# Agent attention with routed experts on one core: GpSimd's chain instructions in halves, strays marked, threshold set and expert loaded later, tiles 13 to 15 of three batches as float16 pairs

## The chip, the cores and the metric

One core of a Trainium2 chip runs the whole program. The metric is the device time of one execution in microseconds (us). Its engines are TensorE (PE in the profile, its weight loads PEld), VectorE (DVE), ScalarE (ACT), GpSimd (POOL) and SyncE (SP), which only issues transfers. Each engine takes its instructions in one fixed order.

## What is computed

For each of B = 4 batches of N = 11456 rows of width 128 there is attention through A = 49 agents, and after it a mixture of E = 8 experts in which each row goes to one expert:

```python
a2k = sm(agents, k); agent_v = a2k @ v          # sm: softmax of scaled scores
x = sm(q, agents) @ agent_v                      # then all batches as rows x
logits = normalized(x) @ normalized(emb).T / tau
e = argmax(logits); gate = softmax(logits)[e]
out = gate * (relu(x @ w1[e]) @ w2[e])           # D = 128, F = 1024
```

## The kernel before, in words

**Tiles.** A batch is 23 tiles (NT) of 4 x 128 rows, the last of 2 x 96; two tiles make a unit, the piece that is loaded, transposed and scored at once. A tile has TICKS = 4 ticks, a tick two half-steps. Every stage is a generator that yields the half-steps to wait (an argument `g` of `pick_expert` is 0 for batch 0 and 1 for the others), and the order in which they emit instructions is the priority from which a scheduler, with times of its own, fixes each engine's order before anything runs. SP's order is exactly the order of emission. `tc.issue_after` (through `in_place`) puts an instruction behind another on the same engine.

**The expert chain.** `pick_expert` runs once per batch, beside the tiles of the batch before (for batch 0 ahead of all tiles). All rows of a batch are expected at one expert, and its hidden units are ordered so that two blocks of 128 are computed exactly and the others are taken as linear: `load_expert` (L885 to L889) loads w1 and w2 into w1s and w2s (one buffer each, SP's queue). The hidden weights gp (L710) give ordering keys (L755 to L770, small DVE operations). From them come diag (L772, POOL for batches 1 to 3), nkey and sgn (L774, L775, DVE), the matmuls `row` (L784), the ranks (L793, L795), the selection sel (L801), and gh and gl (L809 to L819), without which the tiles of this batch do not begin. POOL also makes the low half of gt (L790), scales w2s (L735) and makes the low half of w2x (L736). The linear part lin (L838 to L846) and the placed second layer w2p (L856 matmuls, L858 copied on DVE) follow, then an all-partition maximum (`allmax`: transpose mT L214, DVE reduction mTx L216, matmul mB L219), the threshold thr (L871), 8 instructions sel (L875) and vm (L880). vm serves the proofs.

**Tiles of the expert.** `ffn_mm1` makes hp (L1211, L1212) and the hidden hh. For tiles under LATE = 13, and for all of batch 3, hh is a pair of float16 (ACT L1220, DVE L1221), and `ffn_mm2` does three float16 products per hidden block f (2) and 128 rows (4): L1247 to L1249. Tiles from 13 on of batches 0 to 2 (`plain`) keep hh in float32 (ACT L1216) and do one float32 product with w2f (L1244), which the chip issues as two instructions. L1235 adds the linear part, `ffn_out` scales on DVE (ot, L1263) and stores.

**Proofs and strays.** `proved` (L1056, L1059, L1062, L1065) checks that the linear part holds for each row; `mark_strays` (L1082 to L1182, small DVE operations and L1084 on POOL) marks rows that fail or go to another expert, after the batch's last proof and, half-way, once the next batch has its w2p. `fix` computes a batch's marked rows again: it loads the expert, gathers the rows (`gather`, POOL), waits 24 half-steps and runs `answer` (L1351 with w1s, L1357 with w2s). `stray_first` runs `stray` once, with a load of its own, before fix of batches 2 and 3.

**Other work in the same engines.** Units of q are transposed on PE (L425), scored (L438) and exponentiated, split by POOL (e, L931), transposed by a DMA of SP's queue (tt, L935) and routed (L946, L947). Units of k for batches 2 and 3 are half of them split into float16 pairs (`k1_pairs`, L489 on DVE).

## Time and profile before

| what | value |
|---|---|
| median of three runs | 700.36 us (696.67 to 705.64) |
| the profiled execution: its time / its span | 699.89 us / 698.1 us |
| PE, DVE, ACT, POOL busy | 652.2, 535.5, 453.6, 355.1 us |
| mean granted TensorE clock | 0.969 |

The span runs from the first to the last instruction; 1.8 us lie around it. A clock of 1.0 is the level of 2.4 GHz, 0.5 the level of 1.2 GHz. Batch 0's tile 0 is scaled (ot) at 102 us, its tile 22 at 255, batch 1's at 429, batch 2's at 575, batch 3's at 688.

### The profile page before, as it was taken

The numbers are of one execution on the slowest core, as the hardware profiler recorded it, in microseconds if no ns is written. First come the engines' busy times: TensorE is split into PE (matmuls) and PEld (weight loads), VectorE is DVE, ScalarE is ACT, GpSimd is POOL, SyncE is SP. The second block draws the span as 40 slices with busy tenths as digits, with TensorE's granted clock in tenths as the row PEclk, the third lists the DMA queues.
The fourth block names the chain that finished last, engine by engine and source line by source line (L and its number), as shares of the span: only waits on it lengthen the run. The fifth ranks groups of instructions, "written<-read, shape, count | busy, mean of one in ns | idle before, by whom it ended". The sixth has DMA issues, their size and how long they took to land. (4 is left out here: it accounts for less than half of the span.)

```text
span 698.1 us, 23174 instructions
## 1 busy us (share of the span) xinstructions
PE 652.2 (93%) x9227; PEld 557.9 (80%) x9227; DVE 535.5 (77%) x1470; ACT 453.6 (65%) x1127; POOL 355.1 (51%) x606
## 2 busy tenths in 40 slices
PE   8998999999998888989999888999999999996996
PEld 6886888888887767878889677888888798775876
DVE  5767796878686988876767888977657889985983
ACT  3538746966887636847688853776577857992632
POOL 6002382675153745873533484685645656876410
PEclk9999999999999989989999997999999999998999
DMA  8995596699692267996959245998575424205141
GB/s 342 281 341 174 133 287 169 144 277 238 204 252 69 62 173 194 303 255 160 256 147 221 83 106 136 267 279 204 151 170 169 113 65 114 59 17 171 54 147 70
DMA packets 157047, 123.16 MB, mean 176 GB/s; under 512 B 76787, under 2 KB 133191, under 8 KB 156939
## 3 DMA queue, kind: packets, MB, share of 16 engines
q1 hardware_dynamic: 143499, 97.97, 55.5%
q10 hardware_dynamic: 13120, 23.47, 9.7%
q8 instruction: 73, 1.20, 0.7%
q14 instruction: 35, 0.29, 0.1%
q0 software_dynamic: 320, 0.24, 0.1%
HBM read 80.26 MB, written 23.79 MB: 149 GB/s over the span
## 5 line engine op out<-in xcount | busy, mean ns | idle before, releaser
L1065 ACT ACTIVATE vp<-vp 128x512 f32<-128x512 f32 x180 | 106.1, 590 | 18.7 <-PE vp L1056 13.1
L1220 ACT ACTIVATE hh<-hp 128x512 f16<-128x512 f32 (+1 forms) x124 | 72.4, 591 | 51.7 <-PE hp L1212 30.7
L438 PE MATMUL sp<-aT_all,fT 128*64 128x49 f32 x2496 | 96.4, 226 | 3.4 <-DVE avx L543 2.0
L1221 DVE SCALAR_TENSOR_TENSOR hh<-hp,hh 128x512 f16<-128x512 f32 (+1 forms) x124 | 82.9, 674 | 21.1 <-ACT hh L1220 18.6
L438 PEld LDWEIGHTS sp<-aT_all,fT 128*64 128x64 f32 x2496 | 84.3, 139 | 16.3 <-issue 3.6
L1247 PE MATMUL yp<-w2p,hh 128*128 128x128 f16 (+1 forms) x492 | 95.0, 223 | 0.1
L1248 PE MATMUL yp<-w2p,hh 128*128 128x128 f16 (+1 forms) x492 | 94.9, 223 | 0.0
L1249 PE MATMUL yp<-w2p,hh 128*128 128x128 f16 (+1 forms) x492 | 93.7, 223 | 0.0
L1056 PE MATMUL vp<-vm,tt 128*128 128x256 f16 x360 | 71.0, 274 | 3.9 <-DVE vmin L1062 2.3
L931 POOL TENSOR_TENSOR e<-qe,e 128x392 f16<-128x392 f32 (+1 forms) x48 | 42.2, 880 | 63.3 <-ACT e L928 62.2
L1211 PE MATMUL hp<-tt,gh 128*128 128x512 f16 (+1 forms) x184 | 69.5, 378 | 3.9 <-DVE hh L1221 1.6
L1263 DVE TENSOR_TENSOR ot<-yp,gs 128x512 f32<-128x512 f32 (+1 forms) x92 | 61.2, 668 | 14.6 <-PE yp L1244 8.7
L430 ACT COPY fT<-fTp 128x512 f32<-128x512 f32 (+1 forms) x103 | 57.0, 569 | 23.6 <-PE fTp L425 19.7
L1006 POOL TENSOR_TENSOR nrm<-qq,half 128x16 f32<-128x16 f32 (+2 forms) x28 | 69.9, 2498 | 0.2
L1212 PE MATMUL hp<-tt,gl 128*128 128x512 f16 (+1 forms) x184 | 69.3, 377 | 0.0
L1235 PE MATMUL yp<-lin,tt 128*128 128x128 f16 x720 | 64.9, 224 | 4.5 <-DVE ot L1263 4.4
L1244 PE MATMUL yp<-w2f,hh 128*128 128x128 f32 (+1 forms) x456 | 66.3, 283 | 0.0
L1244 PEld LDWEIGHTS yp<-w2f,hh 128*128 128x128 f32 (+1 forms) x456 | 60.0, 195 | 4.3 <-issue 0.8
L1235 PEld LDWEIGHTS <-tt 128*128 128x128 f16 x720 | 51.1, 102 | 12.3 <-issue 6.0
L425 PE MATMUL fTp<-ident,qt 128*128 128x128 f32 x360 | 55.0, 284 | 1.2 <-ACT hh L1216 0.9
L1247 PEld LDWEIGHTS <-hh 128*128 128x128 f16 (+1 forms) x492 | 49.4, 100 | 4.4 <-ACT hh L1220 0.3
L963 POOL TENSOR_TENSOR rt<-qe 128x392 f32<-128x392 f32 (+1 forms) x48 | 38.4, 800 | 28.2 <-ACT qe L923 20.1
(371 smaller groups left out, 1713.3 us busy)
## 6 DMA issues: line engine op xcount, KB each, us to landing
kt<-in_k_dram SPq DMA_DIRECT2D x44, 512.0 KB, 5.9
vt<-in_v_dram SPq DMA_DIRECT2D x44, 512.0 KB, 7.3
qt<-in_q_dram SPq DMA_DIRECT2D x44, 512.0 KB, 5.2
out_dram<-ot ACTq DMA_DIRECT2D x88, 256.0 KB, 2.3
w1s<-in_moe_w_dram SPq DMA_DIRECT2D x9, 512.0 KB, 5.2
w2s<-in_moe_w_dram SPq DMA_DIRECT2D x9, 512.0 KB
tt<-e SPq DMA_TRANSPOSE x48, 5.2
kt<-in_k_dram SPq DMA_DIRECT2D x4, 96.0 KB, 3.8
```

The lines of the kernel that those rows point to most:

```text
L438: pe.matmul(out=s[h : h + w, c * A : (c + 1) * A], lhsT=xT[:, c * p + h : c * p + h + w], rhs=aT_all[:, b, :], start=True, stop=True, skip ...
L1006: pool.tensor_tensor(out=nrm, in0=quad, in1=half[:, :n], op=ALU.pow)
L1056: pe.matmul(out=z[:p, i * FP : (i + 1) * FP], lhsT=tt[:, c * p : (c + 1) * p], rhs=bt.vm[:, LO:], start=True, stop=True)
L1065: act.activation(z[:p], z[:p], AF.Relu, scale=-1.0, accum_out=bt.vsum[:p, at : at + 1])
L1211: pe.matmul(out=hp[:, :m], lhsT=bt.gh[:, fs], rhs=tt, start=True, stop=False)
L1220: h_last[:] = [act.activation(hh[:, :m], hp[:, :m], AF.Relu)]
L1221: dve.scalar_tensor_tensor(out=hl[:, :m], in0=hp[:, :m], scalar=0.0, in1=hh[:, :m], op0=ALU.max, op1=ALU.subtract)
L1235: pe.matmul(out=yp[:p, c, :], lhsT=tc_, rhs=bt.lin[:, h], start=(c == 0 and h == 0), stop=False, skip_group_check=True)
L1244: y_last[:] = [pe.matmul(out=y, lhsT=hh[:, cs], rhs=bt.w2f[:, f], start=False, stop=last, skip_group_check=True)]
L1247: pe.matmul(out=y, lhsT=hh[:, cs], rhs=wh, start=False, stop=False, skip_group_check=True)
L1248: pe.matmul(out=y, lhsT=hh[:, cs], rhs=wl, start=False, stop=False, skip_group_check=True)
L1249: y_last[:] = [pe.matmul(out=y, lhsT=hl[:, cs], rhs=wh, start=False, stop=last, skip_group_check=True)]
```

## The change

Tiles 13 to 15 of batches 0 to 2 become float16 pairs (LATE 16). The POOL instructions L735, L736, diag and the low half of gt are issued as two halves each, and for batches 1 to 3 L735, L736 and gt stand behind diag in POOL's order; nkey and sgn are emitted before diag. w2p of batches 1 to 3 is copied by ACT. For those batches the transpose mT starts two half-steps later, mB three more, both behind the last emitted product of `ffn_mm2` on PE, and so thr, L875 and vm follow five half-steps later. `mark_strays` waits for the next batch's vm instead of its w2p. `fix` gathers first and loads the expert after its 24 half-steps. L489 is issued in two halves.

```diff
--- before.py
+++ after.py
@@ -43,7 +43,7 @@
     AT = {0: 0, 2: 1}
     BRISK = 4
     KEEP = 5
-    LATE = 13
+    LATE = 16
 
     REM_J, REM_P = 2, 96
     J = (N - REM_J * REM_P) // P
@@ -208,15 +208,18 @@
             except StopIteration as s:
                 return s.value
 
-    def allmax(col, n, tag, psx, g, bufs=2):
-
+    def allmax(col, n, tag, psx, g, bufs=2, place=None):
+
+        place = place or nullcontext
         t_ = psx("mT")
-        pe.transpose(out=t_[:n, :P], in_=col, identity=ident)
+        with place():
+            pe.transpose(out=t_[:n, :P], in_=col, identity=ident)
         mx = sm.tile([P, 1], F32, name="mTx", tag="mTx")[:n]
         dve.tensor_reduce(out=mx, in_=t_[:n, :P], axis=AX.X, op=ALU.max)
         yield g
         t_ = psx("mB")
-        pe.matmul(out=t_[:, :n], lhsT=mx.broadcast_to([n, P]), rhs=ident[:n, :n], start=True, stop=True)
+        with place():
+            pe.matmul(out=t_[:, :n], lhsT=mx.broadcast_to([n, P]), rhs=ident[:n, :n], start=True, stop=True)
         r = sm.tile([P, n], F32, name="pm", tag=tag, bufs=bufs)
         act.copy(r, t_[:, :n])
         return r
@@ -486,7 +489,9 @@
             pool.tensor_tensor(out=src[:p, :n], in0=src[:p, :n], in1=sc.unsqueeze(2).broadcast_to([p, n, D]), op=ALU.mult)
             pool.tensor_tensor(out=xs[:p, :n, 1], in0=src[:p, :n], in1=xs[:p, :n, 0], op=ALU.subtract)
         else:
-            dve.scalar_tensor_tensor(out=xs[:p, :n, 1], in0=src[:p, :n], scalar=sc, in1=xs[:p, :n, 0], op0=ALU.mult, op1=ALU.subtract)
+            for c in range(0, n, TJ):
+                cs = slice(c, min(c + TJ, n))
+                dve.scalar_tensor_tensor(out=xs[:p, cs, 1], in0=src[:p, cs], scalar=sc, in1=xs[:p, cs, 0], op0=ALU.mult, op1=ALU.subtract)
         used("k", b, u)
         yield 6
         i = yield from take(x_slots)
@@ -732,11 +737,21 @@
             yield g
             act.activation(w2x[:, :, 0], w2s, AF.Copy, scale=s3)
             if b > 0:
-                pool.tensor_tensor(out=w2s, in0=w2s, in1=s3.unsqueeze(2).broadcast_to([P, NF, D]), op=ALU.mult)
-                pool.tensor_tensor(out=w2x[:, :, 1], in0=w2s, in1=w2x[:, :, 0], op=ALU.subtract)
+                for h in halves:
+                    with in_place(made):
+                        pool.tensor_tensor(out=w2s[:, h], in0=w2s[:, h], in1=s3.unsqueeze(2).broadcast_to([P, NF // 2, D]), op=ALU.mult)
+                        pool.tensor_tensor(out=w2x[:, h, 1], in0=w2s[:, h], in1=w2x[:, h, 0], op=ALU.subtract)
             return s3, i3
 
         mean, key, nkey, sgn, pw = col("mean"), col("key"), col("nkey"), col("sgn"), col("pw")
+
+        made = []
+        halves = [slice(0, NF // 2), slice(NF // 2, NF)]
+
+        def signs():
+
+            dve.tensor_scalar(nkey, key, -1.0, None, ALU.mult)
+            dve.tensor_scalar(sgn, mean, 0.0, -0.5, ALU.is_ge, ALU.add)
 
         def order_keys():
 
@@ -769,10 +784,13 @@
             yield 1
             dve.tensor_tensor(out=ki, in0=ki, in1=uid, op=ALU.bitwise_or)
             yield 1
-            vec.tensor_tensor(out=diag, in0=ident.unsqueeze(1).broadcast_to([P, NF, P]),
-                              in1=key.unsqueeze(2).broadcast_to([P, NF, P]), op=ALU.mult)
-            dve.tensor_scalar(nkey, key, -1.0, None, ALU.mult)
-            dve.tensor_scalar(sgn, mean, 0.0, -0.5, ALU.is_ge, ALU.add)
+            if b > 0:
+                signs()
+            for h in halves:
+                made[:] = [vec.tensor_tensor(out=diag[:, h], in0=ident.unsqueeze(1).broadcast_to([P, NF // 2, P]),
+                                             in1=key[:, h].unsqueeze(2).broadcast_to([P, NF // 2, P]), op=ALU.mult)]
+            if b == 0:
+                signs()
 
         i2 = yield from (beside(order_keys(), first_scale()) if b == 0 else beside(first_scale(), order_keys()))
         if b > 0:
@@ -787,7 +805,10 @@
             act.copy(row[:, hs], t_)
             yield g
 
-        pool.tensor_tensor(out=gs_[1], in0=gg, in1=gs_[0], op=ALU.subtract)
+        for h in halves:
+            with in_place(made) if b > 0 else nullcontext():
+                pool.tensor_tensor(out=gs_[1][:, 2 * h.start : 2 * h.stop], in0=gg[:, 2 * h.start : 2 * h.stop],
+                                   in1=gs_[0][:, 2 * h.start : 2 * h.stop], op=ALU.subtract)
         rank, more = col("rank"), col("more")
         for c in range(NF // 2):
             dve.tensor_scalar(junk[0], row, key[:, c : c + 1], 0.0, ALU.is_lt, ALU.add, accum_out=rank[:, c : c + 1])
@@ -855,7 +876,7 @@
                 for c in range(NF):
                     pe.matmul(out=t_[:, k_ * 2 * D : (k_ + 1) * 2 * D], lhsT=sel[:, c, (f + k_) * P : (f + k_ + 1) * P],
                               rhs=w2x[:, c].rearrange("p h d -> p (h d)"), start=(c == 0), stop=(c == NF - 1))
-            (act.copy if f % 4 else dve.tensor_copy)(w2p[:, f : f + nk].rearrange("p f h d -> p (f h d)"), t_[:, : nk * 2 * D])
+            (act.copy if b > 0 else dve.tensor_copy)(w2p[:, f : f + nk].rearrange("p f h d -> p (f h d)"), t_[:, : nk * 2 * D])
             yield g
         bt.w2p = w2p
         iall = sm.tile([P, 1], F32, name="iall", tag="iall")
@@ -865,7 +886,8 @@
         bt.iall = iall
         dve.tensor_scalar(rank, rank, -float(FM), None, ALU.add)
         yield 1
-        top = yield from allmax(gmx, 2, "gmxr", psx, 1)
+        yield 2 * g
+        top = yield from allmax(gmx, 2, "gmxr", psx, 1 + 3 * g, 2, lambda: in_place(y_last if b > 0 else []))
         thr = sm.tile([P, 1], F32, name="thr", tag="thr")
         bt.far = sm.tile([P, 1], F32, name="far", tag="far")
         dve.tensor_scalar(thr, top[:, :1], 1.05 * 2.0 ** -11, None, ALU.mult)
@@ -1086,7 +1108,7 @@
         idx = sm.tile([P, NCOL], F32, name="idx", tag="idx", bufs=1)
         dve.tensor_reduce(out=idx, in_=oh, axis=AX.X, op=ALU.min)
         yield 1
-        while b < B - 1 and not hasattr(batches[b + 1], "w2p"):
+        while b < B - 1 and not hasattr(batches[b + 1], "vm"):
             yield 1
         odd = sm.tile([P, NCOL], F32, name="odd", tag="odd", bufs=1)
         ne = sm.tile([P, NCOL], F32, name="ne", tag="ne", bufs=1)
@@ -1376,9 +1398,10 @@
         dve.tensor_scalar(none, bt.fix[:, :1], 0.5, 2 * BIG, ALU.is_lt, ALU.mult)
         yield 1
         dve.scalar_tensor_tensor(out=ix, in0=bt.fix[:, :1], scalar=-1.0, in1=none, op0=ALU.add, op1=ALU.add)
+        xq = gather(ix)
+        yield 24 if b < B - 1 else 0
         w1s, w2s = load_expert(bt.e0i)
-        xq = gather(ix)
-        yield 24 if b < B - 1 else 8
+        yield 0 if b < B - 1 else 8
         yield from answer(xq, ix, bt.fix[:, 1:], aT_all[:, b], av_all[:, b], w1s, w2s, (b + 1) * NT)
         bt.fixed = True
```

## Rows read from the trace of the kernel before

**Rows 1.** The page, part 1: busy us (share of the span) xinstructions of an engine.
```profile
PE 652.2 (93%) x9227; PEld 557.9 (80%) x9227; DVE 535.5 (77%) x1470; ACT 453.6 (65%) x1127; POOL 355.1 (51%) x606
```

**Rows 2.** Busy time by stretch: us, each engine's busy us, clock, DMA share, GB/s.
```profile
147.00:182.00 35.00, 34.96 (x571) 30.50 (x568) 26.18 (x59) 24.59 (x61) 16.63 (x24) 1.00 1.01 238
182.00:205.00 23.00, 23.00 (x301) 20.85 (x300) 15.03 (x49) 18.22 (x46) 8.07 (x13) 1.00 0.91 251
...
510.00:529.50 19.50, 19.50 (x231) 17.65 (x230) 11.50 (x42) 15.73 (x41) 8.68 (x14) 1.00 0.91 226
```

**Rows 3.** Timeline of PE: start, us, instruction; eight float32 instructions, eight float16 products, one.
```profile
207.87 1.05 PE L1244 MATMUL yp<-w2f,hh 128*128 128x128 f32 x8
...
613.37 0.61 PE L1235 MATMUL yp<-lin,tt 128*128 128x128 f16 x8
...
615.30 0.22 PE L1247 MATMUL yp<-w2p,hh 128*128 128x128 f16 x1
```

**Rows 4.** The page, part 5: group | busy us, mean ns | idle before, releaser.
```profile
L1221 DVE SCALAR_TENSOR_TENSOR hh<-hp,hh 128x512 f16<-128x512 f32 (+1 forms) x124 | 82.9, 674 | 21.1 <-ACT hh L1220 18.6 <-issue 1.9
...
L1244 PE MATMUL yp<-w2f,hh 128*128 128x128 f32 (+1 forms) x456 | 66.3, 283 | 0.0
```

**Rows 5.** Timeline of batch 1's keys, DVE, POOL and PE: start, us, [idle before].
```profile
208.41 1.69 POOL L790 TENSOR_TENSOR gt<-gts,gt 128x784 f16<-128x784 f32 x1
208.52 1.62 DVE L768 TENSOR_SCALAR key<-key 128x8 int32<-128x8 int32 x1
...
211.19 0.84 PE L1056 MATMUL vp<-vm,tt 128*128 128x256 f16 x4 [2.26 <-DVE vmin L1062]
```

**Rows 6.** Timeline of batch 2's diag and batch 3's keys: PE, DVE, POOL.
```profile
386.06 0.61 PE L1235 MATMUL yp<-lin,tt 128*128 128x128 f16 x8 [2.17 <-DVE ot L1263]
...
532.01 3.99 DVE L774 TENSOR_SCALAR nkey<-key 128x8 f32<-128x8 f32 x1
...
534.07 1.90 POOL L735 TENSOR_TENSOR w2s<-w2s,hsc 128x1024 f32<-128x1024 f32 x1
```

**Rows 7.** Timeline of the chain's end, DVE in batch 1, PE in batch 2.
```profile
242.98 2.67 DVE L875 TENSOR_SCALAR sel<-iotaf,rank,sgn 128x320 f16<-128x320 f16 x7
245.57 0.68 DVE L858 CAST w2p<-w2pp 128x512 f16<-128x512 f32 x1
...
415.10 2.55 PE L856 MATMUL w2pp<-w1s,sel 128*128 128x256 f16 x16 [2.03 <-DVE qe L921]
421.25 0.58 PE L219 MATMUL mB<-ident,mTx 2*128 2x2 f32 x2 [2.54 <-DVE mTx L216]
```

**Rows 8.** Busy time by stretch: chain ends and after, then stretches at half clock.
```profile
228.00:255.00 27.00, 22.54 (x226) 19.31 (x226) 24.06 (x73) 12.45 (x34) 17.46 (x34) 0.89 0.38 101
400.00:429.00 29.00, 24.43 (x276) 20.19 (x275) 25.68 (x88) 12.92 (x33) 18.69 (x38) 0.82 0.57 137
255.00:282.00 27.00, 25.02 (x446) 21.07 (x444) 23.15 (x68) 16.55 (x44) 12.89 (x34) 0.99 0.81 200
...
211.40:214.80 3.40, 3.40 (x16) 2.91 (x14) 2.20 (x5) 1.83 (x5) 3.40 (x3) 0.50 0.12 43
248.90:255.80 6.90, 6.18 (x36) 5.07 (x38) 5.11 (x22) 1.75 (x5) 1.73 (x5) 0.51 0.65 189
416.20:426.40 10.20, 7.66 (x58) 5.31 (x56) 10.01 (x41) 2.52 (x8) 3.56 (x9) 0.50 0.77 180
634.70:641.50 6.80, 3.75 (x43) 3.66 (x44) 1.94 (x4) 0.69 (x2) 6.09 (x7) 0.50 0.66 222
```

**Rows 9.** Timeline of the last units: POOL, SP's queue (start, us) and PE.
```profile
626.23 0.91 POOL L931 TENSOR_TENSOR e<-qe,e 128x392 f16<-128x392 f32 x1 [0.62 <-POOL rtg L124]
...
628.21 0.35 SPq L888 DMA_DIRECT2D w1s<-in_moe_w_dram  x1
631.01 4.69 SPq L935 DMA_TRANSPOSE tt<-e  x2
...
636.24 0.23 PE L946 MATMUL rtp<-r_hi,tt 128*128 128x58 f16 x1 [4.28 <-DMA tt<-e]
```

## The prediction

> **What bounds the kernel now.** The page's first part comes first: PE is busy for 652.2 of 698.1 us, so 46 us without a matmul are all that better order can give, besides the clock; DVE is next with 535.5 [rows 1]. The view of busy time by stretch then says where PE is full. In the later tiles of a batch it is (34.96 of 35 us, 23.00 of 23.0, 19.50 of 19.5), at full clock, and there only less PE work shortens the time [rows 2]. At the end of an expert chain it is not: 22.54 of 27 and 24.43 of 29 us, with DVE at 24.06 and 25.68 [rows 8]. So DVE, or a wait behind it, sets these stretches. Last the timeline, for what ended PE's longer gaps: DVE in the key chain (2.26 and 2.17 us) [rows 5, 6], DVE at the chain's end (2.03, 2.54) [rows 7], a transpose late on SP's queue near the end (4.28) [rows 9]. After each such place but one the clock stands at 0.50, the level of 1.2 GHz, for 3.4 to 10.2 us [rows 8].
>
> The sums below are made against the profiled execution, 699.89 us (its span and 1.8 us around it); the median of the runs shown, 700.36, lies 0.5 above.
>
> **Tiles 13 to 15.** Nine tiles change, each with 2 hidden blocks by 4 row groups: 72 products. In float32 a product is two instructions; eight take 1.05 us [rows 3], the last 0.28 of it [rows 4], so they stand (1.05 - 0.28) / 7 = 0.110 us apart, 0.220 a product. Eight float16 products of the same shape take 0.61, the last 0.22 of it: 0.056 apart, three make 0.167 [rows 3]. PE saves 72 x 0.053 = 3.8 us, 1.3 per batch, where it is full. DVE gets 18 instructions L1221 of 0.674 us: 12.1 us, 4.0 per batch [rows 4]. It has the room: from 182 to 205, batch 0's tiles 13 to 15, it is busy for 15.03 of 23 us, and 4.0 more make 83%; in batch 2's, 11.50 + 4.0 of 19.5 make 79% [rows 2]. The nearest row for such tiles as pairs is 147 to 182, with DVE at 26.18 of 35 (75%) and PE at 34.96: the cover holds there. It is gone if hp's buffer, now free after ACT, is held by a late L1221; then the ends are 3.8 gained and 12.1 - 3.8 = 8.3 lost. I take 3 gained, nearest to the stretch of pairs.
>
> **The key chain and GpSimd.** In batch 1 the 8-element L768 takes 1.62 us, and it ends 0.04 us after POOL's L790, which began 0.11 us before it; the vmin behind it on DVE is what PE waited for, 2.26 us [rows 5]. The clock is 0.50 from 211.4 to 214.8 with PE busy throughout, which costs half of 3.40, 1.7 us [rows 8]. In batch 2 nkey does the same behind diag, and PE waits 2.17 us for the scaling ot [rows 6]. The change takes both away by order: L790 and L735 go behind diag, so the keys up to diag meet only other POOL work, and nkey goes ahead of diag. Then comes the unhidden side: diag, L790, L735 and L736 now run in one row on POOL, and every DVE instruction that stalls on one will stall on these pieces. What halving does for it the trace bounds from both sides: L768 got in at the end of one POOL instruction [rows 5], so a wait is at most a half, 0.95; nkey in batch 3, at 532.01, took 3.99 us and ended only with L735, the third POOL instruction in a row [rows 6], so halves may give nothing. On POOL only those pieces stand behind diag while it waits for the keys; the POOL work of the q units stays free of that order. The readers of the moved pieces don't become late: row (diag) gets its input earlier, the others are read at the placement and at w2p, 18 us or more later. Ends: 2.26 + 1.7 + 2.17 = 6.1 gained, and nothing gained (where the pieces, one after the other, stop DVE as before); a loss on top isn't excluded, a few tenths for the 4 extra POOL instructions per batch, 1 us in all. I take 3 gained, between the one row that got in and the one that did not.
>
> The Trainium skill (SBUF — State Buffer, "Who interferes with whom") says that GpSimd and a DVE instruction in one of its two-port modes exclude each other for a whole instruction, and that the one issued first goes first. By that rule nkey should have passed after the first POOL instruction and halving would cap each wait at a half; the wait of 3.99 us goes against the last part of the rule [rows 6]. By the rule alone this part would give 4 rather than 3.
>
> **The chain's end.** In batch 1 w2p waits on DVE behind seven L875, 2.67 us, and is copied at 245.57 [rows 7]; by then the PSUM buffer that mT needs is held. In batch 2 the w2p matmuls wait 2.03 us for DVE, busy with marks, and mB, in PE's order ahead of the tiles, waits 2.54 us for its reduction [rows 7]. The change lets ACT copy w2p (12.45 of 27 us busy, so hidden [rows 8]), emits L875 later, puts mB further back in PE's order (behind it stand the tiles, which had to wait with it), and keeps the marks out until vm. The ceiling is all of PE's idle time, 4.46 and 4.57 us, and the half clock: PE is busy 6.18 and 7.66 us there, half of it 6.9; 15.9 in all [rows 8]. DVE is the nearer bound: it is idle for 2.94 and 3.32 us in the two stretches [rows 8], so unless its work leaves they shrink by 6.3. What leaves is w2p's copy (0.68 each) and some 3 us of marks; they come back after vm, where DVE is busy for 23.15 of 27 us [rows 8], so 3 us more just fit. The later threshold makes the proofs of the new batch start some 3 us later, which fills PE less in its first tiles; that is the other end, 3 lost. Batch 3's chain has no such gap. I take 3 gained: half of DVE's bound.
>
> **The loads.** The load in fix of batch 2 (L888) issues at 628.21, once the stray answer has left w1s, and SP's queue is in order: the next transposes issue at 631.01, though POOL finished their input at 627.14 (626.23 + 0.91) [rows 9]. PE waits 4.28 us, then works 3.75 us at half clock [rows 8]. With the load 24 half-steps (three tiles) later the transposes are past it: 631.01 - 627.14 = 3.9 us, and half of 3.75, 1.9: 5.8 at most. Nothing is gained if the end hangs on the last unit, whose input came later than 631 anyhow, or on the last marks. A late load could be waited for by L1351; it has the steps of `answer` ahead of it. I take 2 gained, below the middle. For batches 0 and 1 the same move costs nothing I can see, and the gather moved ahead only starts earlier. Batch 0's chain and the halves of L489 change by tenths: zero, hidden behind PE.
>
> Sum: 3 + 3 + 3 + 2 = 11 us off 699.9 gives 688.9 profiled, 0.5 more against the median: **689.4**, taken as 689.
>
> **The rivals.**
> 1. The gaps form again. DVE is at 89% in both chain ends [rows 8], and each engine's order is made anew, so a PE gap moves to the next late DVE or POOL result; POOL's pieces in a row hold DVE as in batch 3 [rows 6]. For it: nkey's 3.99 us, and DVE's small reserve; against it: the waits named are each removed by order, not by luck. Then only the tiles count: 700.4 - 3.5 = 697.
> 2. All of it goes, the clock too: 3.8 + 6.1 + (6.3 + half of the 6.9 at low clock = 9.8) + 5.8 = 25.5 off 700.4, 675. For it: each half-clock stretch follows a named gap [rows 8]. Against it: 10 us of DVE work are not removed but moved.
> 3. Slower: the pairs tip DVE over. One mechanism: L1221 comes late, hp's buffers stay taken, and PE waits in stretches where it is now full. It decides once DVE's own work in the three stretches reaches PE's: 15.03 + 4.0 against 23 - 1.3 leaves 2.7 us in batch 0 [rows 2], so it takes 3 us of other DVE work or POOL waits that drift in. Price with nothing else gained: 700.4 + 8.3 = 708.7. Against it: 147 to 182 runs so at a full PE [rows 2].
> 4. The change does not do what it says, in one part: two halves back to back act as one instruction. That is 3 us less, 692, inside the forecast's own range.
>
> **How the numbers follow.** Forecast (684 to 694, rival 4 in it) 0.50; gaps form again (694 to 702) 0.25; all goes (672 to 684) 0.15; slower (702 to 712) 0.10. The range that leaves out 2 in 10 is 677 to 703. A measurement of this kernel tells some 2% from no change, here under 686.4 or over 714.4. Faster than that: all of rival 2 and a third of the forecast, 0.15 + 0.17 = 0.32. Slower: the far end of rival 3, 0.03. Within: 0.65.
>
> **What would show it.** Right: tiles 13 to 15 with L1247 to L1249, PE full there, DVE near 80%; L768 and nkey at some 0.17 us, no PE gap over 1 us for vmin or ot in the key chain; w2p copied by ACT right behind its matmuls; no mB gap over 1 us and fewer stretches at 0.50 around the batch changes; L888 of batch 2's fix behind the last transposes on SP, and no gap of 4 us at the last units. Wrong: PE gaps that wait for L1221 in tiles 13 to 15; DVE full for 20 us or more behind each vm with PE waiting for ot; nkey or its followers stretched over several POOL halves; a marks chain of the last batch that ends no earlier against the last tile than now.

## The result, and the profile after

The changed kernel takes 678.62 us (median of four runs, 673.59 to 681.71) where the kernel before took 698.51 beside it (696.35 to 705.64). The ratio is 0.9691, with a 95% interval from 0.9597 to 0.9785: about 3.1% faster, 21.6 us of 698.5. Below, 0.001 of a ratio is 0.7 us. The forecast of 11 us had the sign, and the time lies in its range; the gain is twice as large. The prediction's chances put 0.65 on a change of less than 2% and 0.32 on a faster kernel; the faster kernel came.

The profiled execution took 673.59 us (span 671.3), the shortest of the four, with the highest clock (0.990; the others 0.979 to 0.982). The first part of its page, against [rows 1]:

```profile
PE 635.3 (95%) x9299; PEld 543.4 (81%) x9299; DVE 534.5 (80%) x1498; ACT 453.8 (68%) x1130; POOL 357.6 (53%) x619
```

PE is busy for 16.9 us less. Three terms make up the span: PE's idle time (span less busy), the time that a low clock costs (half of PE's busy time in the stretches at half clock), and what is left, PE's work at full clock. Before, the clock is at 0.50 for 43.0 us in eight stretches, and PE is busy for 34.3 of them; after, for 13.9 us in three (46.4 to 49.8, 244.3 to 251.2, and behind PE's last work), busy for 10.2. So the terms are 45.9 idle, 17.1 for the clock and 635.1 of work before, and 36.0, 5.1 and 630.2 after. Of the 26.8 us between the two profiled executions, 12.0 came from the clock, 9.9 from idle time and 4.9 from work.

For runs without a trace only the span and the mean clock are on record. There the clock's term is taken as the span times one less the clock, which counts idle time at half clock too (21.5 before and 7.0 after, in the profiled executions). Over the four runs it is 11.8 us on average, over 51 runs of the kernel before 20.8, and the rest of the span is 664.0 against 676.8. So in a typical run some 9 us come from the clock and 13 from idle time and work; the profiled execution had more of the clock.

To see where it went, both spans are cut at two events of each expert chain: the end of avT (the last input of `pick_expert`) and the end of the w2p copy, after which the next batch's tiles run freely. The view is busy time by stretch, as in [rows 2]; the second, fourth and sixth lines are the chains of batches 1, 2 and 3. Before:

```profile
0.00:177.50 177.50, 168.70 (x2642) 144.04 (x2643) 132.16 (x345) 110.91 (x258) 75.79 (x155) 0.99 0.87 240
177.50:246.20 68.70, 64.20 (x782) 56.55 (x779) 52.64 (x138) 50.15 (x118) 32.38 (x45) 0.98 0.48 134
246.20:352.90 106.70, 99.66 (x1490) 83.90 (x1491) 82.84 (x218) 66.62 (x169) 59.82 (x105) 0.94 0.86 222
352.90:420.70 67.80, 60.69 (x741) 52.46 (x738) 53.72 (x142) 49.95 (x116) 35.23 (x51) 0.97 0.59 143
420.70:507.60 86.90, 85.95 (x1337) 73.05 (x1338) 68.36 (x192) 54.01 (x144) 54.05 (x97) 0.97 0.83 206
507.60:569.90 62.30, 60.79 (x708) 53.01 (x707) 45.14 (x122) 48.90 (x121) 35.15 (x50) 1.00 0.52 139
569.90:698.10 128.20, 112.24 (x1537) 94.92 (x1535) 100.66 (x320) 73.02 (x203) 62.69 (x106) 0.95 0.30 89
```

After:

```profile
0.00:176.60 176.60, 168.34 (x2643) 143.54 (x2644) 131.13 (x348) 111.65 (x258) 76.33 (x157) 0.99 0.88 241
176.60:236.20 59.60, 57.24 (x733) 49.99 (x732) 49.37 (x133) 48.67 (x113) 29.91 (x43) 1.00 0.56 156
236.20:341.80 105.60, 100.35 (x1574) 85.80 (x1573) 89.17 (x235) 68.69 (x177) 64.22 (x110) 0.97 0.89 224
341.80:401.30 59.50, 57.45 (x754) 50.00 (x752) 50.42 (x140) 48.93 (x116) 31.91 (x50) 1.00 0.61 159
401.30:488.60 87.30, 84.06 (x1345) 71.43 (x1345) 70.13 (x199) 54.16 (x147) 57.25 (x102) 1.00 0.85 210
488.60:545.30 56.70, 56.40 (x709) 49.13 (x707) 40.99 (x121) 47.75 (x117) 34.90 (x53) 1.00 0.58 148
545.30:671.30 126.00, 111.47 (x1556) 93.47 (x1554) 103.34 (x327) 73.92 (x208) 63.04 (x108) 0.99 0.33 91
```

The chains are 9.1, 8.3 and 5.6 us shorter: 198.8 became 175.8 in sum. PE's idle time in them fell from 4.50 + 7.11 + 1.51 = 13.1 to 2.36 + 2.05 + 0.30 = 4.7 us, and the clock rose from 0.97 or 0.98 to 1.00. It rose behind them too: 0.94 to 0.97, 0.97 to 1.00, 0.95 to 0.99. The places that the prediction named, against [rows 5 to 9], in the timeline (start, us, instruction, idle before):

```profile
205.15 0.82 DVE L783 TENSOR_SCALAR key<-key 128x8 int32<-128x8 int32 x1
206.54 0.87 DVE L753 TENSOR_SCALAR nkey<-key 128x8 f32<-128x8 f32 x1
207.33 2.04 POOL L790 TENSOR_TENSOR sel<-ident,key 128x512 f32<-128x512 f32 x2
208.43 2.12 PE L802 MATMUL row<-sel,ones 128*128 128x512 f32 x4 [0.52 <-POOL sel L790]
...
233.71 1.91 PE L877 MATMUL w2pp<-w1s,sel 128*128 128x256 f16 x16
235.65 0.58 ACT L879 CAST w2p<-w2pp 128x512 f16<-128x512 f32 x1 [1.47 <-PE w2pp L877]
...
242.18 0.38 PE L1233 MATMUL hp<-tt,gh 128*128 128x512 f16 x1 [1.81 <-DVE fT L431]
244.43 0.58 PE L222 MATMUL mB<-ident,mTx 2*128 2x2 f32 x2 [1.66 <-DVE mTx L218]
...
617.01 0.36 SPq L910 DMA_DIRECT2D w1s<-in_moe_w_dram  x1
617.32 0.23 PE L968 MATMUL rtp<-r_hi,tt 128*96 128x58 f16 x1 [0.22 <-DMA tt<-e]
```

In batch 1 the key before diag takes 0.82 us instead of 1.62, and the 2.26 us gap for vmin is gone. diag's two halves begin at 207.33 and take 2.04 us together; row starts 1.1 us after that, so right behind the first of them. The sign that the prediction gave for these keys, some 0.17 us, did not come in batch 1. w2p is copied by ACT 0.03 us after its last matmul, at 235.65 instead of 245.57. mB still waits 1.66 us, and a half-clock stretch (244.3 to 251.2) stays behind it. Near the end the load (L910) stands behind the last transposes, and PE waits 0.22 instead of 4.28 us.

### The profile page after: what moved, and what is told of

Same layout as the page of the kernel before. It is cut to its first block, busy times and chain, and to the rows that moved or that the text cites. A ratio compares the mean times of both kernels' runs of the same rounds, so it can differ in the third digit from the quotient of the medians.

```text
span 671.3 us, 23349 instructions
## 1 busy us (share of the span) xinstructions
PE 635.3 (95%) x9299; PEld 543.4 (81%) x9299; DVE 534.5 (80%) x1498; ACT 453.8 (68%) x1130; POOL 357.6 (53%) x619
## 5 line engine op out<-in xcount | busy, mean ns | idle before, releaser
L1242 ACT ACTIVATE hh<-hp 128x512 f16<-128x512 f32 (+1 forms) x142 | 82.8, 589 | 55.1 <-PE hp L1234 23.2
L1243 DVE SCALAR_TENSOR_TENSOR hh<-hp,hh 128x512 f16<-128x512 f32 (+1 forms) x142 | 95.7, 677 | 24.7 <-ACT hh L1242 24.2
L1269 PE MATMUL yp<-w2p,hh 128*128 128x128 f16 x564 | 106.8, 220 | 0.2 <-ACT hh L1242 0.2
L1270 PE MATMUL yp<-w2p,hh 128*128 128x128 f16 x564 | 106.9, 219 | 0.0
L1271 PE MATMUL yp<-w2p,hh 128*128 128x128 f16 x564 | 104.9, 220 | 0.0
L1269 PEld LDWEIGHTS <-hh 128*128 128x128 f16 x564 | 55.6, 99 | 6.9 <-ACT hh L1242 0.6
L1271 PEld LDWEIGHTS <-hh 128*128 128x128 f16 x564 | 55.4, 98 | 5.5 <-issue 0.2
L1257 PEld LDWEIGHTS <-tt 128*128 128x128 f16 x720 | 48.8, 99 | 11.8 <-issue 5.6
L1270 PEld LDWEIGHTS <-hh 128*128 128x128 f16 x564 | 55.3, 98 | 3.6 <-issue 0.2
L985 POOL TENSOR_TENSOR rt<-qe 128x392 f32<-128x392 f32 (+1 forms) x48 | 40.1, 835 | 30.0 <-ACT qe L945 20.2
```

The source lines that it names most:

```text
L1242: h_last[:] = [act.activation(hh[:, :m], hp[:, :m], AF.Relu)]
L1243: dve.scalar_tensor_tensor(out=hl[:, :m], in0=hp[:, :m], scalar=0.0, in1=hh[:, :m], op0=ALU.max, op1=ALU.subtract)
L1257: pe.matmul(out=yp[:p, c, :], lhsT=tc_, rhs=bt.lin[:, h], start=(c == 0 and h == 0), stop=False, skip_group_check=True)
L1269: pe.matmul(out=y, lhsT=hh[:, cs], rhs=wh, start=False, stop=False, skip_group_check=True)
L1270: pe.matmul(out=y, lhsT=hh[:, cs], rhs=wl, start=False, stop=False, skip_group_check=True)
L1271: y_last[:] = [pe.matmul(out=y, lhsT=hl[:, cs], rhs=wh, start=False, stop=last, skip_group_check=True)]
```

## The experiments

The change is taken as six parts: **pairs** (LATE 16), **POOL** (halves, the order behind diag, signs before diag), **end** (w2p on ACT, mT, mB and the threshold later), **marks** (they are to wait for vm), **load** (later in `fix`), and L489 in halves, which was not tried by itself. None of the kernels leaves out any of the computation. First, one part of the changed kernel is taken back; then parts are put into the kernel before, alone and together.

**Pairs taken back (e1).**

```diff
-    LATE = 16
+    LATE = 13
```

> The changed kernel with tiles 13 to 15 of three batches in float32 again (LATE 13), all else as changed. Theory A (the parts add up, each at its own place): 72 products cost 3.8 us more on PE where it is full, so about 3.5 us slower than the changed kernel, near 682 beside 678.6, no more. Theory B (the pairs carry the gain, by keeping PE's clock up through the batch changes): 10 us slower or more, near 690, with half-clock stretches back.

679.42 us, ratio 0.9692 [0.9631, 0.9754] against 0.9691 for the whole change: no gain of the pairs shows in company, though 3 us lie within the intervals.

**Load taken back (e3).**

```diff
+        w1s, w2s = load_expert(bt.e0i)
         xq = gather(ix)
-        yield 24 if b < B - 1 else 0
-        w1s, w2s = load_expert(bt.e0i)
-        yield 0 if b < B - 1 else 8
+        yield 24 if b < B - 1 else 8
```

> The changed kernel with fix's expert loaded ahead of the gather and of its 24 half-steps, as before. Theory A: SP's queue is held again before the last transposes, the 4 us gap and the half clock near the end come back: 4 to 6 us slower than the changed kernel, 683 to 685. Theory B (the end hangs on the last marks or the last unit): within 1.5 us of the changed kernel.

690.54, 0.9856 [0.9795, 0.9917]: 11.5 us of the gain go by the ratios, far more than the 5.8 that the gap near the end could be worth. The chains stay short (176.9 us in sum). What grows are the stretches behind them: 110.8, 92.3 and 131.5 us against 105.6, 87.3 and 126.0. The first of them holds the load of batch 0's `fix`, costed at nothing. The busy time of 10 us there, with the early load:

```profile
270.00:280.00 10.00, 8.10 (x103) 6.47 (x101) 7.07 (x14) 4.71 (x14) 5.51 (x10) 0.84 1.15 323
```

and in the changed kernel, where the load follows at 293.40:

```profile
270.00:280.00 10.00, 9.40 (x149) 7.46 (x147) 9.52 (x31) 6.10 (x19) 6.23 (x9) 1.00 1.15 324
```

PE does 103 instead of 149 matmuls, in part at half clock. But that is not the load holding SP's queue. PE's wait in this stretch is for ACT, and it ends before the load issues (timeline of PE and SP with the early load):

```profile
275.93 0.23 PE L1269 MATMUL yp<-w2p,hh 128*128 128x128 f16 x1 [1.54 <-ACT hh L1242]
275.96 0.37 SPq L910 DMA_DIRECT2D w1s<-in_moe_w_dram  x1
```

From 274 us on PE, DVE and ACT have another order of instructions than in the changed kernel, so this run holds the effect of a new order as well as that of the early load, and does not tell them apart.

**POOL (e5) and end (e6) taken back, each by itself.** The first puts back whole instructions in their old order, with nkey and sgn behind diag; the second the copy on DVE and the early threshold:

```diff
-            (act.copy if b > 0 else dve.tensor_copy)(w2p[...], ...)
+            (act.copy if f % 4 else dve.tensor_copy)(w2p[...], ...)
...
-        yield 2 * g
-        top = yield from allmax(gmx, 2, "gmxr", psx, 1 + 3 * g, 2, lambda: in_place(y_last if b > 0 else []))
+        top = yield from allmax(gmx, 2, "gmxr", psx, 1)
```

> The changed kernel with GpSimd's four chain instructions whole, in the order the scheduler chooses, and nkey and sgn behind diag again. Theory A (each part pays for the gap it removes): the key-chain gaps of some 2 us for vmin or ot in batches 1 and 2 come back with a half-clock stretch, nkey takes 1.6 us or more: 4 to 6 us slower than the changed kernel, 683 to 685. Theory B (the gain lies where fewer instructions meet in DVE's and SP's queues after the batch change, in marks and loads): within 2 us. Theory C (any edit makes each engine's order anew, and the differences between orders are as large as the parts): off by several us with gaps at places that this edit does not touch.

> The changed kernel with w2p copied by DVE and the threshold at once behind w2p, as before. Theory A: the mB gap of 2.5 us in batch 2 and a half-clock stretch of 7 to 10 us there come back: 4 to 6 us slower, 683 to 685. Theory B: within 2 us, since mB still waits 1.66 us in batch 1 of the changed kernel.

683.34, 0.9806 [0.9724, 0.9888], and 685.15, 0.9803 [0.9720, 0.9885]. Both lose about 8 us by the ratios, with intervals that overlap that of the whole change, so the size of either loss is open. Without the end, w2p waits on DVE again and mB for its reduction (DVE and PE in batch 2):

```profile
404.41 3.96 DVE L893 TENSOR_SCALAR sel<-iotaf,rank,sgn 128x320 f16<-128x320 f16 x7
408.29 0.68 DVE L876 CAST w2p<-w2pp 128x512 f16<-128x512 f32 x1
409.48 0.58 PE L219 MATMUL mB<-ident,mTx 2*128 2x2 f32 x2 [3.90 <-DVE mTx L216]
```

**Marks taken back (e7); POOL's instructions whole, in the new order (e8).**

```diff
-        while b < B - 1 and not hasattr(batches[b + 1], "vm"):
+        while b < B - 1 and not hasattr(batches[b + 1], "w2p"):
```

```diff
-        halves = [slice(0, NF // 2), slice(NF // 2, NF)]
+        halves = [slice(0, NF)]
```

> The changed kernel with the marks waiting for the next batch's w2p, as before. Theory A: DVE has 3 us of marks at each chain's end again, mB and the first tiles wait for it: 2 to 4 us slower, 681 to 683. Theory B: the marks carry the gain together with the load, since fix starts behind them: 6 us slower or more. Theory C: several us either way.

> The changed kernel with GpSimd's chain instructions whole, but behind diag as in the change, and nkey and sgn ahead of it. Tells halves from order. If order alone removes the waits: within 1.5 us of the changed kernel. If the halves do it: 3 to 5 us slower, with DVE instructions of 1.6 us or more behind L735, L736 or L790.

676.13, 0.9706 [0.9611, 0.9800], and 678.42, 0.9709 [0.9631, 0.9788]. In the first, PE, DVE, POOL and SP have every instruction in the same order as in the changed kernel: there the condition on vm moves nothing, and the run is a second measurement of the same order. What later marks are worth stays untested. In the second, the time can't be told from that of the changed kernel, though several us either way lie within the intervals, and though in batch 2 the whole instructions keep nkey busy for 5.70 us, where the halves make it 0.82 (DVE):

```profile
375.09 5.70 DVE L753 TENSOR_SCALAR nkey<-key 128x8 f32<-128x8 f32 x1
```

**One part alone, in the kernel before.** Pairs (e2), load (e4) and end (e14), by the diffs of e1, e3 and e6 the other way round, and the order of POOL (e13: whole instructions behind diag, signs before it; the definitions and the old signs lines are left out here):

```diff
...
+            if b > 0:
+                signs()
-            vec.tensor_tensor(out=diag, ...)
+            made[:] = [vec.tensor_tensor(out=diag, ...)]
...
-                pool.tensor_tensor(out=w2s, ...)
-                pool.tensor_tensor(out=w2x[:, :, 1], ...)
+                with in_place(made):
+                    pool.tensor_tensor(out=w2s, ...)
+                    pool.tensor_tensor(out=w2x[:, :, 1], ...)
...
-        pool.tensor_tensor(out=gs_[1], in0=gg, in1=gs_[0], op=ALU.subtract)
+        with in_place(made) if b > 0 else nullcontext():
+            pool.tensor_tensor(out=gs_[1], in0=gg, in1=gs_[0], op=ALU.subtract)
```

> The kernel before with LATE 16 alone. Theory A: 3 to 4 us faster than the kernel before, near 695, the key-chain gaps and the half-clock stretches as before. Theory B: 10 us faster or more. Theory C (the pairs fill DVE, which only the rest of the change makes room for): no gain or a few us slower, 699 to 706, with longer PE waits on DVE in the key chain.

> The kernel before with the later load alone. Theory A: no 4.28 us gap at the last units, full clock there, 4 to 6 us faster than before, 693 to 695, the rest of the trace as before. Theory B: within 1.5 us of the kernel before.

> The kernel before with the order of GpSimd's chain instructions alone. If the parts add up: 7 us faster, as much as order gives beside end and load (0.9812 to 0.9705), ratio 0.990; no 2 us gaps for vmin or ot in the key chains of batches 1 and 2. If they need each other: 3 us or less, 0.996 or more, with the gaps moved to the chain's end.

> The kernel before with the chain end alone (w2p on ACT, threshold later). If the parts add up: 7 us faster or more, 0.990 or less, with no mB gap over 2 us in batch 2 and no half-clock stretch of 10 us there. If they need each other: 3 us or less.

Pairs: 695.64, 0.9956 [0.9923, 0.9989], 3.1 us. Load: 698.64, 0.9968 [0.9929, 1.0007], 2.2 us, which can't be told from none. Order: 686.61, 0.9820 [0.9767, 0.9873], 12.6 us. End: 690.83, 0.9857 [0.9810, 0.9904], 10.0 us. With the late load alone the transposes of the last units issue early and the 4.28 us gap for them is gone, but another of the same size stands a little later (PE and DVE):

```profile
641.62 0.69 DVE L1263 TENSOR_TENSOR ot<-yp,gs 128x512 f32<-128x512 f32 x1 [1.05 <-DMA out_dram<-ot]
642.36 1.01 PE L1235 MATMUL yp<-lin,tt 128*128 128x128 f16 x8 [4.24 <-DVE ot L1263]
```

**Inside the order: POOL's order without the signs (e17), and the signs without the order (e18).** The first is the diff above without the signs() lines (nkey and sgn stay behind diag); the second is those lines alone.

> The kernel before with L735, L736 and gt behind diag in POOL's order, nkey and sgn behind diag as before. If the gain comes from diag going first (the row matmuls then get an earlier place in PE's order and the chain ends earlier): most of order's 12.6 us, 0.982 to 0.986, the stretch from avT to w2p 9 us shorter or more over the three batches. If nkey's stall was the cost: 0.995 or more.

> The kernel before with nkey and sgn emitted ahead of diag, POOL's order free. If nkey's stall behind diag was the cost: 4 us faster or more, 0.994 or less, PE's 2.17 us wait for ot in batch 2 gone. If diag's place is what counts: within 2 us of the kernel before, the stretch from avT to w2p no shorter than 2 us in all.

688.76, 0.9842 [0.9805, 0.9880], 11.0 us, and 700.10, 0.9999 [0.9958, 1.0040]. The first has the same order of instructions on every engine as e13, so 12.6 and 11.0 us are two measurements of one order: that of three POOL instructions carries it. The second changes nothing in the trace. PE, DVE, POOL and SP have the order of the kernel before, in which nkey already stood right behind the last key on DVE, and nkey takes as long as in [rows 6]:

```profile
532.63 3.99 DVE L743 TENSOR_SCALAR nkey<-key 128x8 f32<-128x8 f32 x1
```

So that run measures the kernel before once more (PE's waits of some 2 us for vmin and ot are in it too), and does not tell what nkey's stall costs. With POOL's order alone the wait for vmin is gone and the one for ot is 0.95 instead of 2.17 us, though nkey still takes 1.67 us in batch 2. What else changes is the way from avT to row and w2p. In the timeline of the kernel before, batch 1:

```profile
177.26 0.26 DVE L578 TENSOR_TENSOR avT<-foldp,lr 128x98 f32<-128x98 f32 x1
210.42 1.90 POOL L772 TENSOR_TENSOR sel<-ident,key 128x1024 f32<-128x1024 f32 x1 [0.31 <-DVE key L770]
212.68 1.92 PE L1244 MATMUL yp<-w2f,hh 128*128 128x128 f32 x8
...
215.93 0.60 PE L425 MATMUL fTp<-ident,qt 128*128 128x128 f32 x4
...
217.91 1.88 PE L784 MATMUL row<-sel,ones 128*128 128x512 f32 x4
```

With POOL's order alone:

```profile
178.97 0.26 DVE L578 TENSOR_TENSOR avT<-foldp,lr 128x98 f32<-128x98 f32 x1
208.98 0.17 DVE L778 TENSOR_SCALAR key<-key 128x8 int32<-128x8 int32 x1
209.50 1.90 POOL L783 TENSOR_TENSOR sel<-ident,key 128x1024 f32<-128x1024 f32 x1 [0.58 <-DVE key L780]
212.22 1.88 PE L794 MATMUL row<-sel,ones 128*128 128x512 f32 x4
240.39 0.68 DVE L871 CAST w2p<-w2pp 128x512 f16<-128x512 f32 x1
```

Before, diag is done at 212.32 and row, which needs nothing else, starts 5.59 us later: PE, in its fixed order, has another unit's transposes and float32 products first. With the order made anew row starts 0.82 us after diag. Counted from the end of avT, diag is done after 34.8 us before and 32.2 now, row starts after 40.4 and 33.0, w2p is there after 68.7 and 61.8. So the first 2.6 us come from the keys on DVE, which diag waits for and which no longer stall beside L735 and L790 (the last but one takes 0.17 us instead of 1.62 [rows 5]), and 4.8 from PE's order; that the scheduler places row earlier because diag comes early in its own times is likely, but not shown. In batches 2 and 3 w2p comes 1.7 and 3.3 us earlier.

Row's place is not the price by itself. With LATE 16 alone (e2) PE's order is made anew too: row starts 0.05 us behind diag in batch 1, the chains are 190.1 us in sum, 8.8 shorter, and the time is only 3.1 us shorter.

**Two and three parts together.** The edits are the diffs shown: end and load (e10), order and end (e11), order and load (e15), all three (e9; no pairs, no halves, no later marks).

> The kernel before with chain end and load. Theory A (each pays at its place, as the named gaps): 6 for the end and 2 for the load, 8 us faster, 0.988. Theory D (a part pays only when the waits behind it are gone too, so that undoing any one costs most of a larger sum): under 6 us, 0.991 or more, with a new wait where one was removed.

> The kernel before with order and chain end, the load early. Theory A: 5 + 6 = 11 us faster, 0.984. Theory D: it lacks the load, which cost 12 us when undone alone, so no better than 0.983 to 0.988, close to the changed kernel with the load early (0.9856).

> The kernel before with order and load. If the parts add up: order's 7 and the load's 2 to 7, 9 to 14 us faster, 0.980 to 0.987. If they need the chain end: 5 us or less, 0.993 or more.

> The kernel before with three parts alone: order (GpSimd's chain instructions whole, behind diag, nkey and sgn ahead of it), chain end (w2p on ACT, threshold later), load later. No pairs, no halves, no later marks. If these three carry the gain, as the runs that undo one part each say: within 1.5 us of the changed kernel by ratio, 0.968 to 0.973. If the small parts matter in company: 0.975 or more.

The ratios are taken against runs of the kernel before beside each kernel, so they, and not the times, are to be compared.

| parts | us | ratio [95%] | chains in sum, us |
|---|---|---|---|
| none (profile before) | 698.51 | 1 | 198.8 |
| order | 686.61 | 0.9820 [0.9767, 0.9873] | 187.0 |
| end | 690.83 | 0.9857 [0.9810, 0.9904] | 187.5 |
| load | 698.64 | 0.9968 [0.9929, 1.0007] | 198.1 |
| order, load | 681.39 | 0.9732 [0.9683, 0.9780] | 186.9 |
| end, load | 688.35 | 0.9812 [0.9737, 0.9887] | 187.3 |
| order, end | 687.25 | 0.9799 [0.9725, 0.9873] | 177.0 |
| all three | 680.60 | 0.9705 [0.9622, 0.9789] | 175.8 |

The three parts give what the whole change gives. On the chains order and end add up (11.8 and 11.3, together 21.8 us); on the time they don't (0.0180 and 0.0143 would make 0.0323; together it is 0.0201). The matmul counts say why. Order and load, then all three, batch 1's chain and the stretch behind it:

```profile
178.00:239.80 61.80, 60.96 (x772) 54.33 (x769) 46.90 (x135) 50.07 (x118) 31.19 (x42) 1.00 0.54 149
239.80:342.50 102.70, 96.64 (x1509) 81.81 (x1506) 82.44 (x222) 66.64 (x170) 60.42 (x108) 0.98 0.87 231
```

```profile
179.20:238.20 59.00, 58.48 (x710) 52.04 (x708) 44.10 (x126) 48.95 (x114) 28.60 (x39) 1.00 0.56 155
238.20:343.80 105.60, 100.39 (x1590) 85.93 (x1590) 86.58 (x229) 70.96 (x183) 63.14 (x111) 1.00 0.89 227
```

The end takes 62 matmuls out of a chain in which PE was already full (0.84 us idle), and 2.8 us; the next stretch has 81 matmuls more and is 2.9 us longer. By these runs a chain made shorter gains only the idle time and the half clock in and behind it.

Order's worth in the four pairs of the table is 12.6, 16.5, 4.1 and 7.5 us (alone, with the load, with the end, with both), the end's 10.0, 10.9, 1.5 and 1.9 (alone, with the load, with order, with both), each to some 4 to 8 us. So order and end stand in for each other to a large part. Order's worth is positive in all four, and 8 us where it is taken back (e5), so it is hardly the luck of one new order.

The load's worth in the four pairs is 2.2, 6.1, 3.1 and 6.6 us (alone, with order, with the end, with both). The first and third can't be told from none; in the other two every run with the late load is shorter than every run without it, taken beside it. Up to 620 us PE, DVE and POOL have the same order with order alone as with order and load; only SP's queue differs, from 275 us on. Both profiled executions end batch 3's chain at the same time, and the load's gain lies in the last stretch, where the prediction had looked for it. Order alone, from the end of batch 1's chain, without the chain of batch 3, and below it the last stretch with the load:

```profile
239.00:342.10 103.10, 96.61 (x1509) 80.98 (x1504) 82.50 (x220) 66.55 (x170) 60.47 (x108) 0.98 0.88 230
342.10:408.20 66.10, 61.47 (x760) 53.28 (x759) 52.16 (x145) 49.72 (x116) 35.76 (x51) 1.00 0.61 153
408.20:496.40 88.20, 84.94 (x1357) 72.22 (x1357) 68.89 (x191) 56.08 (x150) 55.04 (x97) 1.00 0.84 201
...
555.40:683.30 127.90, 111.33 (x1521) 92.59 (x1518) 101.06 (x318) 72.38 (x202) 63.03 (x106) 0.95 0.32 89
```

```profile
555.30:679.70 124.40, 109.96 (x1521) 91.36 (x1518) 101.76 (x318) 72.02 (x202) 62.60 (x106) 0.97 0.32 91
```

Between order-and-end and all three the last stretch is 128.6 against 125.5 us. The other stretches behind the chains differ too (108.9 and 94.0 against 105.6 and 92.2), but the larger difference is one of the clock ahead of the load: without it the clock is at 0.50 from 242.9 to 249.8, with the same order of instructions on PE, and the load issues at 276.2.

**Inside the end: the three parts, with w2p copied on DVE as before (e16).** The edit leaves the `(act.copy if f % 4 else dve.tensor_copy)` line as it was.

> Order, load and the later threshold, with w2p copied by DVE again. If the copy on ACT matters: 2 us or more slower than the three parts (0.9705), with w2p's copy behind L875 and mT waiting for its buffer. If the later threshold alone does it, since L875 is then emitted after w2p's copy: within 1.5 us.

683.73, 0.9757 [0.9707, 0.9807], chains 187.7: the chains are as long as with order and load alone (186.9), so the later threshold shortens none; the copy on ACT does it. In the time the two can't be told apart from the three parts (0.9705).

**A load four half-steps earlier (e12)** in the changed kernel (`yield 20` and `yield 4` for 24 and 0), meant to be harmless.

> The changed kernel with the expert loaded 20 half-steps late instead of 24, the answer at the same step. Both are past the transposes, so the mechanism of the load is untouched; what it shows is how far a harmless edit moves the time, by the new order that the scheduler makes. Theory A: within 2 us of the changed kernel. Theory C (luck of the order): 4 us or more either way.

684.24, 0.9750 [0.9675, 0.9825]: 4 us slower by the ratios, with overlapping intervals. A new order that nobody meant can so be worth about as much as the pairs or the load alone. The profiled execution lost 7.5 us before the change could matter, with the same order of instructions on every engine up to 286 us, against the first stretch of the changed kernel above:

```profile
0.00:184.10 184.10, 176.61 (x2642) 150.95 (x2643) 130.48 (x348) 111.93 (x258) 76.04 (x157) 0.95 0.84 231
```

No kernel tried beats the changed one beyond the intervals; the simplest that equals it is the one with three parts.

## Why the prediction was right in sign and short in size

**Where it failed.** The step is the sum in "The key chain and GpSimd": "Ends: 2.26 + 1.7 + 2.17 = 6.1 gained", of which 3 were taken. The term was mis-sized: POOL's order alone gave 12.6 and 11.0 us (e13, e17), twice its upper end. The gaps that it names shrink from 4.4 to 0.95 us in those runs, so they hold at most 3.5 us of it. What the sum left out is mainly the clock, of which it priced 1.7 us. Over the eight runs of e13 and e17 the clock's term is 12.1 us where the kernel before has 20.8; the rest of the span is 2.9 us shorter. In both profiled executions of the order before (before, e18) the clock is at 0.50 for 3.4 us behind batch 1's gap for vmin, for 6.8 from 300 on, and for 10.2 and 3.4 us at the end of batch 2's chain; with POOL's order alone none of these is left in either (e13, e17), although DVE still copies w2p. The prediction had priced the last of them under the chain's end [rows 8] and the one at 300 nowhere. The clock columns show it for behind batch 1's chain, batch 2's chain, and behind that: 0.94, 0.97 and 0.97 before, 0.98, 1.00 and 1.00 with POOL's order alone.

A second step of that part was costed at nothing: "row (diag) gets its input earlier". row stood 5.59 us behind diag in PE's order, and w2p came 6.9 us earlier in batch 1's chain once the order was made anew. Idle PE in the three chains fell from 13.1 to 5.6 us, and the named gaps are 3.5 of these 7.5. And "nkey goes ahead of diag" moved nothing (e18). Why each single stretch at 0.50 went away is not settled: no run isolates one, and e2 shows that row's place alone does not do it.

**The chain's end**, taken at 3 between -3 and 15.9, gave 10.0 alone and 1.9 where order and load were there already (which can't be told from none); taken out of the whole change it cost 8 (e6), and no run tells why that is more. The mechanism was right (w2p waiting on DVE), but the half of DVE's bound was the wrong price: copied on ACT, w2p comes 3.2, 5.0 and 3.2 us earlier in its chain, and nothing else in this part shortens it (e16). The later marks, to which 3 of the 6 us of relief were put, moved no instruction (e7). "No mB gap over 1 us" was wrong in batch 1 (1.66).

**The tiles** were right in the working: 72 products in 144 float32 instructions became 72 in three float16 each, L1221's kind came 18 times more, PE is full there, and DVE at 79% and 74% (batches 1 and 2):

```profile
345.60:361.40 15.80, 15.80 (x235) 14.01 (x231) 12.44 (x37) 11.83 (x31) 7.34 (x12) 1.00 0.90 243
492.40:511.80 19.40, 19.40 (x281) 17.53 (x280) 14.34 (x50) 16.52 (x42) 8.88 (x14) 1.00 0.98 238
```

PE's work at full clock, reckoned as in the section on the result, is 634.0 to 637.0 us in the twelve profiled kernels without the pairs and 629.9 to 632.8 in the eight with them, 4.1 less on average where 3.8 were forecast. That the pairs alone gave 3.1 us, as taken, is luck all the same: in the profiled execution of e2 PE's work is 2.5 us less, but its idle time 3.3 us more, and 4.5 us came from the clock, which that sum did not hold. In the whole change no gain is seen in the time, and 3 us are not excluded.

**The load** was taken at 2 of at most 5.8, from one gap. Alone it gave 2.2, and its gap was replaced by one for ot (e4). In company with order it gave 6.1 and 6.6; 3.5 and 3.1 us of that lie in the last stretch, the place that was forecast, and within its bound. "Costs nothing I can see", for batches 0 and 1, is borne out there: order alone and order with load reach the end of batch 3's chain together. Why the early load cost 11.5 us in the changed kernel (e3) is not settled, since that edit made the order anew from 274 us on.

**The halves.** GpSimd's pieces were bounded between nothing and half of a wait. In the time nothing shows, with several us left open (e8). The Trainium skill (SBUF — State Buffer, "Who interferes with whom") says that whichever of GpSimd and a two-port DVE instruction issues first has the shared ports for that whole instruction, by which smaller pieces should shorten DVE's waits. They did in batch 2, where nkey takes 0.82 us instead of 5.70; but 5.70 us is more than any one GpSimd instruction beside it takes (at most 1.90), as the 3.99 us of before were. That DVE's stalls cost nothing isn't shown: those of the keys delayed diag by 2.6 us.

**The rivals.** The time fell into the range of the second (all goes, 672 to 684, at a chance of 0.15), but not by its sum: 6.1 + 9.8 + 5.8 + 3.8 were gaps and their clock, while mB's gap stayed and the order's gain was not in the sum. Gaps that only move (the first) were seen for one part, the load alone. Pairs that tip DVE over (the third) did not happen; in the nine tiles of e2 no wait of PE over 0.2 us ends with L1221. The fourth, halves that act as whole instructions, can't be told from the forecast by time.

## What to carry to other kernels

Where a chain gates the next stage, mark its first input and its last output, and price a change by the idle time and the half clock of PE in and behind that stretch, not by the gaps that have a name; its length alone is no price, since PE's work in it only moves on. Where a scheduler fixes the order ahead, look at what stands on the waiting engine between an operand's end and its reader: here 5.59 us, and moving three instructions of another engine changed it. Look whether an edit moved an instruction at all before its time is read: two edits here did not (e7, e18). And where every edit makes the order anew, a part's worth is safest read between two kernels whose order is otherwise the same, as for the load.

## What the runs showed of the hardware that was not expected

The same first stretch differs from run to run by its clock: up to the end of batch 1's avT the profiled executions took 177.5 us before (clock 0.99), 182.1 with the end alone (0.95) and 184.1 in e12 (0.95), with 2642 or 2643 matmuls in each. Up to there the order on PE is the same in the first two, and the same in e12 and the changed kernel (176.6 us). The difference is as large as several of the parts.

A DVE instruction on 8 elements was stretched to 5.70 us (nkey in batch 2 of e8) and ended 0.02 us after the last of four GpSimd instructions in a row; with these in halves it took 0.82 us. The times of the two kernels can't be told apart (0.9709 and 0.9691), so a stall of that size need not show in the time.
